# Heads 1 to 11 of a clustered attention: probabilities times values as one fp32 product

## The chip, the core and the metric

The program runs on one core of a Trainium2 chip. The metric is the device time of one execution in microseconds (us); the median of the runs is compared. Engines are named as in the profile: PE (TensorE matmul), PEld (its weight loads), DVE (VectorE), ACT (ScalarE), POOL (GpSimd), SP (SyncE, which issues most DMAs).

## What is computed

Three stages follow one another. The first is an attention in which a query sees only the keys whose nearest centroid is its own; the second is a two-layer block with a softmax-weighted unit (SoLU) and a layer norm; the third is a mixture of 8 experts with one expert a token. The change concerns the last line of the first function.

```python
B, H, S, D = 2, 8, 768, 64            # 16 heads in all
mask   = q_assign[:, :, :, None] == k_assign[:, :, None, :]
scores = np.where(mask, q @ k.T / 8, -1e9)
scores = scores - np.max(scores, axis=-1, keepdims=True)
attn   = np.exp(scores)
attn   = attn / (np.sum(attn, axis=-1, keepdims=True) + 1e-09)
return np.matmul(attn, v)             # (768 x 768) times (768 x 64), for each head

h  = x @ w_in;  solu = h * softmax(h);  y = layernorm(solu) @ w_out     # 1536 x 512 -> 1024 -> 512
out = gate * (relu(y_of_expert @ w1[e]) @ w2[e])                        # 8 experts, 512 -> 1024 -> 512
```

## The kernel before

Matmul operands are mostly kept as two fp16 halves: the high half is the value rounded to fp16, the low half is the remainder. A product of two such operands is three fp16 matmuls (high by high, high by low, low by high).

**The order.** All instructions of the attention and of the second stage are added to one `Plan`. Each `add(engine, cost, at, fn, reads, writes, ...)` gives a booked cost and a due time. `emit` plays a list scheduler: it takes at each step the ready operation with the lowest rank, where a rank is worked out from the due time, the length of the way to the end and a correction by kind and stretch from the table `LEAN`. The result is one fixed order for each engine's queue, SP's and POOL's too; the chip runs each queue in that order and waits at semaphores.

**The heads.** They go two at a time (a pair is one DMA of q and k, `prep`). Heads 0 and 12 to 15 go through `late`, in which probabilities are normalised by the row and turned by a DMA transpose. Heads 1 to 11 go through `head`:

- L499 and L502: for each of 6 blocks of 128 queries and 2 halves of the keys, one matmul of 384 columns into a PSUM bank and a DVE maximum over it. The maxima are turned (L511, L515, L517) and written as a row of q.
- L535 and L536: the transposed scores, keys by queries, one fp16 and one single-pass fp32 matmul (type fp32r) of 384 columns each, 12 pairs a head, into the PSUM tiles `psS`.
- L544: ACT takes the exponential of two blocks at a time (768 elements a partition), twice: once into fp16 (`ph`, shown as `pr`), once into fp32 (`pf`).
- L408 (`halves`): POOL subtracts, two instructions of 384 elements for each `pf`, and writes the low half `plo` (also shown as `pr`).
- L557 to L559 (`pv`): for each group of 128 queries, 6 key blocks by 3 fp16 matmuls of 65, 64 and 65 columns accumulate in one PSUM bank. Stationary are the probabilities, moving are the values; column 65 of the values is 1, so that the row sum comes out too. A head has two such groups of three, 6 calls of `pv`; the 11 heads have 66.
- L417 to L420 (`normalise`): DVE divides by the row sum and writes into `X`.

**The values.** L396 loads the fp32 values of a pair into `v32` (one buffer), L398 (ACT) makes their fp16 high half, L401 (DVE, twice a pair) the low half, in `V`.

**Beside them.** While the heads run, DVE, ACT and POOL also prepare the two weight matrices of the second stage (L612, L615 and L618 assemble fp32 words, L622 and L624 make halves, L631 on POOL). From about 180 us on, tiles of the second stage (L720 to L949) run between the later heads. The third stage begins at about 400 us.

Of the kernel before, what the change touches and what calls it, by code (L numbers as in the profile page):

```python
# [41 lines left out]
LEAN = {
    "act V": (0, 213.5, 0), "act bsm": (0, -40.4, 0), "act cw": (0, 0, 37), "act e": (0, -9.2, -1.9),
    "act hi": (221.8, 2.5, 0), "act hr": (1.3, 0, 0), "act lh": (0, 4.7, 0.4), "act ohT": (-1.5, 12.6, 0),
    "act pf": (0.1, -87.6, 0), "act rsm": (0, -0.2, 0), "act vh": (0, 6.2, 0), "act wf": (0, -2.6, 0),
    "act wgh": (3.6, 0, 0), "act wi": (113.4, 0, 0), "act wo": (-3.9, -4.3, 0), "act x1": (0, 6.6, 5.6),
    "act ys": (0, -3.4, -8.6), "dve V": (56.3, 3.7, 0), "dve X": (1.8, 0, 0), "dve acc": (0, -1.4, 0),
    "dve bsm": (0, 16.1, -0.1), "dve cbd": (5.6, 0, 0), "dve cw": (0, 0, 83.7), "dve e": (0, -2.8, -2.8),
    "dve eq": (7.7, -20.9, 0), "dve gs": (-0.7, 0, 0), "dve id": (-19.5, 0, 0), "dve ids": (0, 0, -5.1),
    "dve lo": (10.8, 0, 0), "dve loh": (0, -12, 0), "dve m2": (11.4, 0.6, 0), "dve mv": (4.7, 4.7, 0),  # L50
    "dve mx": (-0.2, 0.2, 0), "dve nm": (0, 6.3, 0), "dve nn": (2, 8.3, 0), "dve oh": (-2.6, -0.5, 0),
    "dve one": (1.6, 0, 0), "dve rn": (-3.7, 0, 0), "dve rr": (-10, 0, 0.5), "dve rsm": (0, -12.9, 0),
    "dve si": (0, 1.8, 0.9), "dve tri": (-6.2, 0, 0), "dve vl": (-6.3, 0.1, 0), "dve wf": (24.5, -1.2, 0),
    "dve wgl": (3.1, 0, 0), "dve wi": (6.9, 0, 0), "dve x1": (0, 0, 0.6), "dve ys": (0, 3.4, 3.4),
# [3 lines left out]
    "pool e": (0, 1.2, 0), "pool half": (6.6, 0, 0), "pool plo": (-0.5, 0, 0), "pool pn": (4.4, 0, 0),  # L58
# [136 lines left out]
def plan_attention(tc, plan, ctx, ps, qkT, vP, cent2, cst, cs, X, ident32, ident16):  # L195
# [3 lines left out]
    v32 = pa.tile([P, 2, NCH, D], F32, tag="v32", name="v32")  # L199
# [17 lines left out]
    ph, plo = [t[:, 0] for t in pr], [t[:, 1] for t in pr]  # L217
# [87 lines left out]
    lifted = ("QK1", 0, 2)

    def prep(p):
# [102 lines left out]
    def normalise(h, g, gv, t):  # L410
        def a3():
# [6 lines left out]
            out=r, in0=a3()[:, :, 64:65], scalar1=1e-9, scalar2=16.0, op0=ALU.add, op1=ALU.mult), reads=[gv], writes=[kr])  # L418
# [5 lines left out]
    def late(h):  # L424
# [10 lines left out]
        for c in range(NCH):  # L435
# [19 lines left out]
            old = ([] if first >= 7 else [(x, (2 * EH) % 3, i) for x in ("ph", "plo") for i in range(3)] if first < 3  # L455
# [861 lines left out]
```

## Time and profile before

| | us |
|---|---|
| median of 3 runs (lowest, highest) | 576.39 (576.3, 579.86) |
| the profiled execution | 580.83 |
| its span, first to last instruction | 579.1 |
| PE busy in the span | 506.7 (87%) |
| DVE busy | 417.3 (72%) |
| ACT busy | 368.1 (64%) |
| PEld busy | 326.7 (56%) |
| POOL busy | 278.3 (48%) |

The profiled execution lies 4.4 us above the median, and its span 2.7 us above it. Busy shares are means over stages with different limits, so they are read by stage. A busy PE is not a PE at its peak: the end of a matmul record is modelled, and records overlap. What a matmul costs its queue is read from the distance of the starts of two that follow each other.

### The profile page before, as it was taken

The numbers are of one execution on the slowest core, as the hardware profiler recorded it, in microseconds if no ns is written. First come the engines' busy times: TensorE is split into PE (matmuls) and PEld (weight loads), VectorE is DVE, ScalarE is ACT, GpSimd is POOL, SyncE is SP. The second block draws the span as 40 slices with busy tenths as digits, with TensorE's granted clock in tenths as the row PEclk, the third lists the DMA queues.
The fourth block names the chain that finished last, engine by engine and source line by source line (L and its number), as shares of the span: only waits on it lengthen the run. The fifth ranks groups of instructions, "written<-read, shape, count | busy, mean of one in ns | idle before, by whom it ended". The sixth has DMA issues, their size and how long they took to land.

```text
span 579.1 us, 13110 instructions
## 1 busy us (share of the span) xinstructions
PE 506.7 (87%) x4945; PEld 326.7 (56%) x4945; DVE 417.3 (72%) x976; ACT 368.1 (64%) x553; POOL 278.3 (48%) x292
## 2 busy tenths in 40 slices
PE   1478889889688898998889999988979999999995
PEld 1255666667565464654554445465727675675672
DVE  7499899999989899987755999963653445645110
ACT  3466788888767889986745989823544434635120
POOL 2057798999878758888752443520000101011001
PEclk9998899999979999999999999999979999999999
DMA  8898858796879799999999778948986573964300
GB/s 245 198 200 212 261 175 228 204 277 171 165 187 224 151 215 165 204 217 187 218 204 229 205 189 200 276 109 206 285 312 174 218 248 135 318 186 164 73 7 17
DMA packets 159340, 113.75 MB, mean 196 GB/s; under 512 B 126560, under 2 KB 135074, under 8 KB 159268
## 3 DMA queue, kind: packets, MB, share of 16 engines
q1 hardware_dynamic: 156660, 106.31, 74.8%
q0 software_dynamic: 2320, 6.32, 3.1%
q8 instruction: 46, 0.75, 0.5%
q14 instruction: 26, 0.21, 0.1%
q10 hardware_dynamic: 288, 0.16, 0.1%
HBM read 51.57 MB, written 17.11 MB: 119 GB/s over the span
## 4 chain that ended last, share of the span: by engine, by line
DVE 28%; issue 24%; DMA 23%; PE 14%; ACT 4%; POOL 4%; SPq 3%; POOLq 1%; ACTq 0%; DVEq 0%
DMA out_dram<-yo,ids 10%; DVE mm L502 6%; DMA pr<-pn 3%; DVE wf L615 2%; DVE hl L324 2%; PE psb L499 2%; DMA xs<-ys,si 2%; DVE mm L449 1%; DVE wf L618 1%; SPq L1024 1%; DMA wgs<-in_wg_dram 1%; DVE wf L612 1%; PE psS L446 1%; PE psS L445 1%; PE psS L535 1%
## 5 line engine op out<-in xcount | busy, mean ns | idle before, releaser
L408 POOL TENSOR_TENSOR pr<-pf,pr 128x384 f16<-128x384 f32 x168 | 173.0, 1060 | 54.9 <-ACT pr L460 27.6
L1084 POOL DMA_INDIRECT out_dram<-yo,ids x16 | 17.4, 1085 | 160.5 <-ACT yo L1081 153.5
L1057 PE MATMUL psb<-cxT,ah 128*128 128x256 f16 (+1 forms) x288 | 71.8, 261 | 1.5 <-DMA cxT<-xs 1.5
L1059 PE MATMUL psb<-cxT,al 128*128 128x256 f16 (+1 forms) x288 | 71.8, 261 | 0.9 <-PEq L1158 0.8
L1058 PE MATMUL psb<-cxT,ah 128*128 128x256 f16 (+1 forms) x288 | 71.8, 261 | 0.0
L502 DVE TENSOR_REDUCE mm<-psb 128x1 f32<-128x384 f32 x132 | 67.0, 546 | 4.9 <-PE psb L499 4.5
L1071 DVE SCALAR_TENSOR_TENSOR hl<-psb,hh 128x512 f16<-128x512 f32 x32 | 21.9, 689 | 58.3 <-ACT hh L1070 41.6
L991 DVE SCALAR_TENSOR_TENSOR al<-w,ah 128x1024 f16<-128x1024 f32 x32 | 40.5, 1279 | 29.2 <-ACT ah L990 29.1
L536 PE MATMUL psS<-QK 96*128 96x384 f32 x132 | 60.6, 494 | 0.0
L544 ACT ACTIVATE pf<-psS 128x768 f32<-128x768 f32 x66 | 53.1, 804 | 9.6 <-PE psS L536 5.7
L499 PE MATMUL psb<-QK 96*128 96x384 f32 x132 | 47.5, 416 | 13.3 <-DVE mm L502 9.8
L544 ACT ACTIVATE pr<-psS 128x768 f16<-128x768 f32 x66 | 52.6, 803 | 6.7 <-PE psS L536 6.2
L1076 PE MATMUL psb<-bh,hh 128*128 128x512 f16 x128 | 49.7, 388 | 3.2 <-ACT hh L1070 3.2
L1078 PE MATMUL psb<-bh,hl 128*128 128x512 f16 x128 | 49.8, 389 | 0.7 <-DVE hl L1071 0.7
L1077 PE MATMUL psb<-bl,hh 128*128 128x512 f16 x128 | 49.6, 388 | 0.0
L535 PE MATMUL psS<-QK 128*128 128x384 f16 x132 | 45.9, 348 | 1.7 <-ACT pr L544 1.0
L557 PE MATMUL psb<-V,pr 128*128 128x65 f16 x396 | 43.4, 196 | 3.6 <-DVE mm L502 3.1
L990 ACT ACTIVATE ah<-w 128x1024 f16<-128x1024 f32 x32 | 33.0, 1052 | 21.3 <-DMA w<-in_w_dram 20.5
L559 PE MATMUL psb<-V,pr 128*128 128x65 f16 x396 | 43.2, 194 | 1.1 <-POOL pr L408 1.1
L1070 ACT ACTIVATE hh<-psb 128x512 f16<-128x512 f32 x32 | 18.9, 592 | 38.6 <-PE psb L1059 38.4
L558 PE MATMUL psb<-V,pr 128*128 128x64 f16 x396 | 43.2, 197 | 0.0
L991 DVE SCALAR_TENSOR_TENSOR bl<-w,bh 128x1024 f16<-128x1024 f32 x32 | 39.0, 1230 | 5.8 <-ACT bh L990 4.6
(193 smaller groups left out, 1557.6 us busy)
## 6 DMA issues: line engine op xcount, KB each, us to landing
w<-in_w_dram SPq DMA_DIRECT2D x64, 512.0 KB
xs<-X SPq DMA_DIRECT2D x12, 516.0 KB
QK<-hr SPq DMA_DIRECT2D x16, 384.0 KB
QK<-hl SPq DMA_DIRECT2D x32, 192.0 KB
x<-in_qkT_dram SPq DMA_DIRECT2D x7, 768.0 KB
lT<-in_w_in_dram SPq DMA_DIRECT2D x8, 512.0 KB
lT<-in_w_out_dram SPq DMA_DIRECT2D x8, 512.0 KB
v<-in_vP_dram SPq DMA_DIRECT2D x8, 384.0 KB
```

Source lines behind the costliest of these rows:

```text
L408: nc.gpsimd.tensor_tensor(out=out[:, i], in0=a[:, i], in1=b[:, i], op=ALU.subtract)
L499: add("pe", 0.18, at(c - 10 + 0.25 * g), lambda c=c, g=g, w=w: nc.tensor.matmul(w.bank[:, :384], q1[:, c * P : (c + 1) * P], k1[:, g * 384 ...
L502: add("dve", 0.465, at(c - 9.9 + 0.25 * g), lambda c=c, g=g, w=w: nc.vector.tensor_reduce(out=m2[mm][:, c, g : g + 1], in_=w.bank[:, :384] ...
L535: nc.tensor.matmul(o, k2[:, ks], q2[:, qs], start=True, stop=False)
L536: nc.tensor.matmul(o, k1[:, ks], q1[:, qs], start=False, stop=True)
L544: add("act", 0.691, at(k + 0.5), lambda dst=dst, kb=kb: nc.scalar.activation(dst, ps[kb][:, :, :384], AF.Exp, scale=SC), reads=[kb], write ...
L991: run("dve", lambda: nc.vector.scalar_tensor_tensor(out=W[e][kl][:, gs], in0=box[0], scalar=64.0, in1=W[e][kh][:, gs], op0=ALU.mult, op1=A ...
L1057: nc.tensor.matmul(o, w["ah"][:, c, fs], x[:, 0, c, ts], start=(c == 0), stop=False)
L1058: nc.tensor.matmul(o, w["ah"][:, c, fs], x[:, 1, c, ts], start=False, stop=False)
L1059: nc.tensor.matmul(o, w["al"][:, c, fs], x[:, 0, c, ts], start=False, stop=(c == KC - 1))
L1076: nc.tensor.matmul(y, hh[:, f, i], w["bh"][:, f], start=(f == 0), stop=False)
L1078: nc.tensor.matmul(y, hl[:, f, i], w["bh"][:, f], start=False, stop=(f == FC - 1))
```

## The change

In `head` the fp16 exponential and the low half are gone: ACT writes one fp32 exponential per two blocks, straight into the space that `ph` and `plo` had, and `pv` multiplies the fp32 probabilities by the fp32 values in one matmul in place of three. The value tile has a column of ones of its own and two buffers; pairs 1 to 5 no longer make `V`. The scale 16 of the halves falls away in `normalise`. Heads 0 and 12 to 15 stay as they were, but for their waits: each wait for `ph` and `plo` is one for `ph` now. The booked cost of a `pv` is 0.8 in place of 0.5, and every entry of `LEAN` is another, so that all engines' orders are new. The diff, with most of `LEAN` and the two places of `late` left out:

```diff
@@ -38,28 +38,33 @@
 FIRST, LATE = 18, 8
+PV = 0.8
 MARKS = (48, 93,)
 LEAN = {
-    "act V": (0, 213.5, 0), "act bsm": (0, -40.4, 0), "act cw": (0, 0, 37), "act e": (0, -9.2, -1.9),
...
+    "act V": (-16.4, 37.6, 0), "act bsm": (0, 40.7, -22.6), "act cc": (169.2, 0, 0), "act cs": (54.1, 0, 0),
...
 }
@@ -196,7 +201,7 @@
     nc, add = tc.nc, plan.add
     pa = ctx.enter_context(tc.tile_pool(name="pa", bufs=1))
     x32 = pa.tile([P, 2, S], F32, tag="x32", name="x32")
-    v32 = pa.tile([P, 2, NCH, D], F32, tag="v32", name="v32")
+    v32 = ring(pa, "v32", 2, [P, 2, NCH, D + 1], F32)
     hl = ring(pa, "hl", 2, [P, 4, S], F16)
     hr = pa.tile([P, 2, S], F32R, tag="hr", name="hr")
     QK2 = ring(pa, "QK2", 2, [P, 2, S], F16)
@@ -214,7 +219,7 @@
     rn = mm_[:, 44:45]
     nmt = ring(pa, "nmt", 2, [NCH, P], F32R)
     pr = ring(pa, "pr", 3, [P, 2, NCH, 384], F16)
-    ph, plo = [t[:, 0] for t in pr], [t[:, 1] for t in pr]
+    ph = [t.rearrange("p a c t -> p (a c t)").bitcast(F32).rearrange("p (c t) -> p c t", c=NCH) for t in pr]
     E0, EH, E4 = 1, 12, 12 % 4
 
     def parts(t, n):
@@ -301,6 +306,7 @@
     for i in range(2):
         add("pool", 0.35, -90.0, lambda i=i: nc.gpsimd.memset(oh[i], 0.0), writes=[("oh", i)])
         add("pool", 0.1, -80.0, lambda i=i: nc.gpsimd.memset(V[i][:, :, :, 64:65], 1.0), writes=[("V1", i)])
+        add("pool", 0.1, -80.0, lambda i=i: nc.gpsimd.memset(v32[i][:, :, :, 64:65], 1.0), writes=[("v1", i)])
 
     lifted = ("QK1", 0, 2)
 
@@ -393,14 +399,17 @@
                     out=QK2[d2][64 * half : 64 * half + 64], in_=hl[b][r, 1:3] if half else hl[b][r, 0:4:3]),
                     reads=[(nm, b, t) for nm in ("hi", "lo") for t in range(2)] + ([lifted] if h == 1 or (h == 0 and 0) else []),
                     writes=[("QK2", d2, half)] + ([("neg", h)] if half and not E0 <= h < EH else []), data=0.2)
-        add("sp", 0.65, at(-10), lambda: nc.sync.dma_start(out=v32, in_=vP[p]),
-            reads=[("neg", 2 * p - 1)] if p else [], writes=["v32"], data=0.39)
-        add("act", 0.73, at(-2), lambda: nc.scalar.activation(V[b][:, :, :, 0:64], v32, AF.Copy, scale=16.0),
-            reads=["v32", ("oh", 0)], writes=[("V", b, 0), ("V", b, 1)])
+        v = v32[b][:, :, :, 0:D]
+        add("sp", 0.65, at(-8 if p else -10), lambda: nc.sync.dma_start(out=v, in_=vP[p]),
+            reads=[("neg", 2 * p - 1)] if p else [], writes=[("v32", b)], data=0.39)
+        if E0 <= 2 * p and 2 * p + 1 < EH:
+            return
+        add("act", 0.73, at(-2), lambda: nc.scalar.activation(V[b][:, :, :, 0:64], v, AF.Copy, scale=16.0),
+            reads=[("v32", b), ("oh", 0)], writes=[("V", b, 0), ("V", b, 1)])
         for j in range(2):
             add("dve", 0.47, at(-1), lambda j=j: nc.vector.scalar_tensor_tensor(
-                out=V[b][:, j, :, 65:129], in0=v32[:, j], scalar=16.0, in1=V[b][:, j, :, 0:64],
-                op0=ALU.mult, op1=ALU.subtract), reads=["v32"], writes=[("V", b, j)])
+                out=V[b][:, j, :, 65:129], in0=v[:, j], scalar=16.0, in1=V[b][:, j, :, 0:64],
+                op0=ALU.mult, op1=ALU.subtract), reads=[("v32", b)], writes=[("V", b, j)])
 
     def halves(out, a, b):
 
@@ -415,7 +424,8 @@
         r, kr = rr[u % 2], ("rr", u % 2)
         t0, hh = (h // H) * NCH + 3 * g, h % H
         add("dve", 0.07, t, lambda: nc.vector.tensor_scalar(
-            out=r, in0=a3()[:, :, 64:65], scalar1=1e-9, scalar2=16.0, op0=ALU.add, op1=ALU.mult), reads=[gv], writes=[kr])
+            out=r, in0=a3()[:, :, 64:65], scalar1=1e-9, scalar2=1.0 if E0 <= h < EH else 16.0, op0=ALU.add, op1=ALU.mult),
+            reads=[gv], writes=[kr])
         add("dve", 0.09, t, lambda: nc.vector.reciprocal(out=r, in_=r), writes=[kr])
         add("dve", 0.27, t, lambda: nc.vector.tensor_tensor(
             out=X[:, t0 : t0 + 3, hh * D : (hh + 1) * D], in0=a3()[:, :, 0:64], in1=r.to_broadcast([P, 3, D]), op=ALU.mult),
...
@@ -537,30 +547,20 @@
 
                 add("pe", 0.326, at(k + 0.3 * (c % 2)), sT,
                     reads=kqk + [("QK1", d, 4 + g), ("QK2", d2, 0), ("QK2", d2, 1)], writes=[kb])
-                fb = n % 3
-                old = free.get(u, [])
                 if c % 2:
-                    for dst, key in ((ph[ub][:, c - 1 : c + 1], ("ph", ub, c // 2)), (pf[fb], ("pf", fb))):
-                        add("act", 0.691, at(k + 0.5), lambda dst=dst, kb=kb: nc.scalar.activation(
-                            dst, ps[kb][:, :, :384], AF.Exp, scale=SC), reads=[kb], writes=[key] + (old if key[0] == "ph" else []))
-                if c % 2:
-                    add("pool", 1.6, at(k + 0.8), lambda c=c, fb=fb, ub=ub: halves(
-                        plo[ub][:, c - 1 : c + 1], pf[fb], ph[ub][:, c - 1 : c + 1]),
-                        reads=[("pf", fb), ("ph", ub, c // 2)], writes=[("plo", ub, c // 2)])
+                    add("act", 0.691, at(k + 0.5), lambda c=c, ub=ub, kb=kb: nc.scalar.activation(
+                        ph[ub][:, c - 1 : c + 1], ps[kb][:, :, :384], AF.Exp, scale=SC),
+                        reads=[kb], writes=[("ph", ub, c // 2)] + free.get(u, []))
             gv = Hold()
             for qc in range(3):
                 def pv(qc=qc, ub=ub, gv=gv):
                     A = gv.bank[:, qc * 65 : qc * 65 + 65]
-                    v = V[b]
                     qs = slice(qc * P, (qc + 1) * P)
                     for c in range(NCH):
-                        nc.tensor.matmul(A, ph[ub][:, c, qs], v[:, j, c, 0:65], start=(c == 0), stop=False)
-                        nc.tensor.matmul(A[:, :64], ph[ub][:, c, qs], v[:, j, c, 65:129], start=False, stop=False)
-                        nc.tensor.matmul(A, plo[ub][:, c, qs], v[:, j, c, 0:65], start=False, stop=(c == NCH - 1))
-
-                add("pe", 0.5, at(3 * g + (2.9 + 0.1 * qc if h == EH - 1 else 4.5 + 0.8 * qc)), pv,
-                    reads=[("ph", ub, i) for i in range(3)] + [("plo", ub, i) for i in range(3)]
-                    + [("V", b, j), ("V1", b)], writes=[gv], get=None if qc else gv)
+                        nc.tensor.matmul(A, ph[ub][:, c, qs], v32[b][:, j, c], start=(c == 0), stop=(c == NCH - 1))
+
+                add("pe", PV, at(3 * g + (2.9 + 0.1 * qc if h == EH - 1 else 4.5 + 0.8 * qc)), pv,
+                    reads=[("ph", ub, i) for i in range(3)] + [("v32", b), ("v1", b)], writes=[gv], get=None if qc else gv)
             normalise(h, g, gv, at(3 * g + 6.3))
 
     for p in range(NPAIR):
```

## Rows read from the trace of the kernel before

**Rows 1.** Windows: us, busy PE, PEld, DVE, ACT, POOL, clock, DMA share.
```profile
60.00:150.00 90.00, 80.85 (x1136) 61.28 (x1136) 87.75 (x185) 75.97 (x105) 83.00 (x80) 0.98 0.78 226
150.00:180.00 30.00, 23.71 (x280) 17.40 (x279) 27.70 (x49) 22.52 (x33) 24.90 (x23) 0.83 0.74 165
180.00:240.00 60.00, 53.19 (x620) 32.13 (x619) 55.40 (x138) 51.50 (x87) 45.33 (x47) 1.00 0.96 184
240.00:310.00 70.00, 61.95 (x755) 36.99 (x754) 51.26 (x182) 48.41 (x78) 50.44 (x59) 1.00 1.13 205
310.00:410.00 100.00, 94.98 (x754) 51.38 (x751) 77.25 (x257) 67.24 (x125) 32.47 (x33) 1.00 0.80 208
```

**Rows 2.** Groups by line, 60-150 us: xcount | busy, mean ns | idle.
```profile
L408 POOL TENSOR_TENSOR pr<-pf,pr 128x384 f16<-128x384 f32 x80 | 84.5, 1088 | 7.0 <-ACT pf L544 5.5 <-PE psb L499 1.3
L502 DVE TENSOR_REDUCE mm<-psb 128x1 f32<-128x384 f32 x84 | 42.4, 546 | 1.8 <-PE psb L499 1.6
...
L499 PE MATMUL psb<-QK 96*128 96x384 f32 x82 | 27.1, 380 | 6.2 <-DVE mm L502 5.5 <-DMA QK<-ohT 0.3 <-ACT nmt L517 0.2
...
L324 DVE SCALAR_TENSOR_TENSOR hl<-x,hl 128x768 f16<-128x768 f32 x6 | 8.5, 1432 | 0.0
...
L624 DVE SCALAR_TENSOR_TENSOR il<-wf,ih 128x512 f16<-128x512 f32 x6 | 6.4, 1066 | 0.1
L615 DVE SCALAR_TENSOR_TENSOR wf<-lT,wf 128x512 int32<-128x512 int32 x5 | 5.9, 1176 | 0.0
L618 DVE SCALAR_TENSOR_TENSOR wf<-lT,wf 128x512 int32<-128x512 int32 x5 | 5.2, 1044 | 0.0
...
L401 DVE SCALAR_TENSOR_TENSOR V<-v,V 128x384 f16<-128x384 f32 x6 | 4.6, 774 | 0.0
```

**Rows 3.** Groups by line, whole span.
```profile
L544 ACT ACTIVATE pf<-psS 128x768 f32<-128x768 f32 x66 | 53.1, 804 | 9.6 <-PE psS L536 5.7 <-POOL pr L408 3.6
...
L398 ACT ACTIVATE V<-v 128x768 f16<-128x768 f32 x8 | 6.7, 844 | 0.0
```

**Rows 4.** Single lines: xcount, ns min/median/max, first and last start.
```profile
L324 DVE SCALAR_TENSOR_TENSOR hl<-x,hl x16: 928/1053/1671, 7.7 to 204.6; 128x768 f16<-128x768 f32 x16
L615 DVE SCALAR_TENSOR_TENSOR wf<-lT,wf x16: 693/1256/1402, 14.9 to 221.8; 128x512 int32<-128x512 int32 x16
L618 DVE SCALAR_TENSOR_TENSOR wf<-lT,wf x16: 676/914/1401, 15.6 to 223.8; 128x512 int32<-128x512 int32 x16
L624 DVE SCALAR_TENSOR_TENSOR il<-wf,ih x8: 675/900/1403, 26.0 to 149.9; 128x512 f16<-128x512 f32 x8
```

**Rows 5.** Timeline, PE, 84-90 us: start, duration, line.
```profile
84.81 0.32 PE L535 MATMUL psS<-QK 128*128 128x384 f16 x1
...
85.15 0.34 PE L535 MATMUL psS<-QK 128*128 128x384 f16 x1
...
87.42 0.19 PE L557 MATMUL psb<-V,pr 128*128 128x65 f16 x1
...
87.94 0.19 PE L559 MATMUL psb<-V,pr 128*128 128x65 f16 x1
87.96 0.42 PE L499 MATMUL psb<-QK 96*128 96x384 f32 x1
```

**Rows 6.** Timeline, PEld, 85.8-86.5 us.
```profile
85.94 0.30 PEld L499 LDWEIGHTS psb<-QK 96*128 96x128 f32 x2
86.40 0.10 PEld L535 LDWEIGHTS <-QK 128*128 128x128 f16 x1 [0.16 <-issue]
```

**Rows 7.** Single lines, transposes on PE: columns as in rows 4.
```profile
L365 PE MATMUL psb<-ident,oh x48: 217/219/330, 13.7 to 227.1; 128*128 128x128 f16 x48
L515 PE MATMUL psb<-ident,mm x11: 271/273/402, 42.6 to 187.9; 128*6 128x128 f32 x11
L297 PE MATMUL psb<-ident,pf x1: 444/444/444, 6.1 to 6.1; 128*128 128x128 f32 x1
```

**Rows 8.** DMA queue of SP: packets, MB, share of 16 engines.
```profile
q1 hardware_dynamic: 156660, 106.31, 74.8%
```

More of the change, by code (lines that the diff above doesn't have):

```diff
@@ L40 @@
 FIRST, LATE = 18, 8
+PV = 0.8
 MARKS = (48, 93,)
 LEAN = {
-    "act V": (0, 213.5, 0), "act bsm": (0, -40.4, 0), "act cw": (0, 0, 37), "act e": (0, -9.2, -1.9),
[L44 to L52, printed above, removed]
@@ L53 @@
-    "dve si": (0, 1.8, 0.9), "dve tri": (-6.2, 0, 0), "dve vl": (-6.3, 0.1, 0), "dve wf": (24.5, -1.2, 0),
-    "dve wgl": (3.1, 0, 0), "dve wi": (6.9, 0, 0), "dve x1": (0, 0, 0.6), "dve ys": (0, 3.4, 3.4),
[3 rows of a table removed]
-    "pool e": (0, 1.2, 0), "pool half": (6.6, 0, 0), "pool plo": (-0.5, 0, 0), "pool pn": (4.4, 0, 0),
[4 rows of a table removed]
+    "act V": (-16.4, 37.6, 0), "act bsm": (0, 40.7, -22.6), "act cc": (169.2, 0, 0), "act cs": (54.1, 0, 0),
+    "act cw": (0, 0, 409.8), "act e": (0, 0, 126.2), "act hi": (-50.9, 163.3, 0), "act hr": (8.7, 3.8, 0),
@@ new lines @@
+    "act lh": (0, 256, -0.4), "act nmt": (-5.8, -20.4, 0), "act ohT": (-21.2, -92.1, 0), "act pf": (-0.5, 17.8, 0),
+    "act ph": (-33.8, 123.2, 0), "act pn": (0.6, -1.6, 0), "act rsm": (0, 18.2, -13.9), "act vh": (-17.4, -74.5, 0),
+    "act wf": (9.4, 266.8, 0), "act wi": (-2.9, 0, 0), "act wo": (25.1, -25.6, 0), "act x1": (0, 266.1, -0.6),
+    "act ys": (0, 9.9, 36.2), "dve V": (28.7, 0, 0), "dve X": (91.2, 94, -47.8), "dve acc": (0, 5.2, 15.9),
+    "dve bsm": (0, -3.8, -517.5), "dve cbd": (-6.2, 0, 0), "dve cnt": (0, 0, 57.9), "dve cw": (0, 0, -23),
@@ new lines @@
+    "dve e": (0, 403.7, 1.3), "dve eq": (28.5, 40.5, 0), "dve gs": (-30.8, 0, 0), "dve id": (-3.9, 0, 0),
+    "dve ids": (0, 0, 33.9), "dve lo": (0, -6.8, 0), "dve loh": (0, 34.9, -86.3), "dve m": (17.7, -74.5, 0),
+    "dve m2": (168.2, -0.7, 0), "dve mv": (0, 81.6, 0), "dve mx": (61, 3.7, 0), "dve nm": (29.6, -59.3, 0),
+    "dve nn": (-0, -13.5, 0), "dve oh": (0.1, 7.9, 0), "dve one": (63.3, 0, 0), "dve rn": (22.6, 0, 0),
+    "dve rr": (153.9, -24.5, -1), "dve rsm": (0, 123.6, -102.1), "dve si": (0, 79.1, 1.8), "dve tie": (-111.7, 0, 0),
@@ L63 @@
+    "dve tri": (-31.6, 0, 0), "dve vl": (-34.6, -234.9, 0), "dve wf": (617.7, -1, 0), "dve wgl": (-1, 0, 0),
[4 rows of a table added]
+    "pool X": (-35.4, 0, 0), "pool bsm": (0, -9, 45), "pool e": (0, 92.7, -7.4), "pool half": (4.6, 0, 0),
+    "pool id32": (-8.3, 0, 0), "pool oh": (-1.1, 0, 0), "pool pn": (11.1, -0.6, 0), "pool ring": (0, -27, 8.3),
+    "pool rn": (3.5, 0, 0), "pool v1": (25, 0, 0), "pool wo": (-20.9, 48.1, 0), "pool ysi": (0, 4.1, 14.7),
[4 rows of a table added]
 }
@@ L454, in late @@
                 reads=[("nm", h % 2, c)], writes=[("nn", h % 2, c), ("m2", h % 2, c, 1)])
-            old = ([] if first >= 7 else [(x, (2 * EH) % 3, i) for x in ("ph", "plo") for i in range(3)] if first < 3
+            old = ([] if first >= 7 else [("ph", (2 * EH) % 3, i) for i in range(3)] if first < 3
                    else [("more", (first - 3) // 2)])
@@ L464, in late @@
                 reads=[("pf", fb), ("pn", ib, 0)], writes=[("pn", ib, 1)])
-            old = [(x, (2 * EH + 1 + ub) % 3, i) for x in ("ph", "plo") for i in range(3)] if first < 6 else []
+            old = [("ph", (2 * EH + 1 + ub) % 3, i) for i in range(3)] if first < 6 else []
             add("sp", 1.69, at(o + 0.7), lambda c=c, ib=ib, ub=ub: nc.sync.dma_start(
```

15 rows, old and new, of the table LEAN are left out of this document.

## The prediction

> **What bounds the kernel now.** I read the busy time by stage first, because shares of the whole span mix stages. From 60 to 150 us, where the heads run almost alone, DVE is busy 87.75 of 90 us and POOL 83.0, while PE's records cover 80.9 and ACT 76.0 [rows 1]. Then I read the groups by line in that stretch. It holds 84 DVE maxima of L502 and 84 is 7 x 12, so exactly 7 heads pass, one in 12.86 us. DVE waits there almost for nobody, while PE's L499 waits 5.5 us for DVE's L502 to free a bank [rows 2]. POOL's subtractions of L408 take 1088 ns each; 12 a head are 13.1 us, as long as a head [rows 2]. So two engines are full at once. The single lines tell that they are full partly of each other: the DVE operations with two inputs in SBUF have minima of 0.68 to 0.93 us [rows 4] and means of 1.04 to 1.43 us in this stretch [rows 2], while L502, which reads PSUM, keeps 546 ns. The reader is to see that a DVE operation beside L408 pays for L408.
>
> PE has to be read by starts. A pv call of 18 fp16 matmuls runs from 87.42 to 87.96, 0.54 us, 30 ns a matmul; a pair of L535 and L536 takes 85.15 - 84.81 = 0.34 us [rows 5], so one matmul of 384 columns about 0.17. A head's PE work is then 12 x 0.17 + 12 x 0.34 + 6 x 0.54 = 9.4 us. The 128 other matmuls of the stretch (1136 less 7 x 144 [rows 1, 5]) at 30 ns add 0.55 a head: 9.9 of 12.86 us. PE has some 3 us a head to spare, although its records look full.
>
> Later the limits change. From 180 to 240 us PE is busy 53.2 of 60 and DVE 55.4; from 240 to 310 the DMA share is 1.13; from 310 to 410 PE is busy 95.0 of 100 [rows 1].
>
> **The change part by part.** *POOL* loses 11 x 12 = 132 of its L408, at 1088 ns 144 us [rows 2]. *ACT* loses the 66 exponentials into pf, 53.1 us, and 5 of 8 conversions of the values, 5 x 0.844 = 4.2 us [rows 3]; the pv calls need not wait for POOL behind ACT any more. POOL and ACT then have room everywhere in the heads, so these two terms count only through DVE.
>
> *DVE* loses L401 for five pairs; 6 of them are in the stretch, 4.6 us [rows 2]. The contention goes with L408: mean less minimum is 6 x (1432 - 928) + 6 x (1066 - 675) + 5 x (1176 - 693) + 5 x (1044 - 676) ns = 3.0 + 2.3 + 2.4 + 1.8 = 9.6 us [rows 2, 4]. POOL keeps L631 and some work of the second stage, so between 0 and 9.6 us comes back; I take all of it for this stretch, since hardly any other POOL work lies in it. DVE goes from 87.75 to 73.6 us for 7 heads, 10.5 us a head.
>
> *PE* loses 66 calls at 0.54 us and gets 66 calls of six fp32 products each. No row shows such a product, and this is the open price. An fp32 transpose of 128 columns takes 273 ns where an fp16 one takes 219 [rows 7]: 54 ns more, so fp32 columns pass at half the pace. A load of weights in 4-byte form takes longer too: two of them merged take 0.30 us, one fp16 load 0.10 [rows 6]. If a single one takes 0.19, the second began 0.11 us after the first, so one load holds the path for 0.11. That gives three prices. With all loads hidden and one load a product, 6 x 0.11 = 0.66 us a call. With two loads a product, one for the upper and one for the lower bits, 6 x 0.22 = 1.3 us. With nothing overlapped, six times the only fp32 matmul with 128 x 128 weights in the trace, 444 ns [rows 7], 2.7 us. I take 0.8, near the lower end. The reason is the kernel's own bookings, which agree with the starts within 8%: 0.5 booked against 0.54 for the old pv call, 0.326 against 0.34 for a pair [rows 5]; the new call is booked at 0.8. That is weak, so both ends stay in the range, the third as a tail.
>
> The Trainium skill speaks against the change here. Its page "FP8 and Floating Point Precision", section "TensorE Precision Notes", says a true fp32 product is four passes through the array; by the 30 ns of a pass that is an estimate of 0.12 us a product, 0.72 a call, and the sum below would come out some 5 us lower. Its page "TensorE: Matmul & The Clock Gate", section "Weight-path perf modes", says that fast weight load is off for fp32 weights. The slower fp32r loads agree with that, but no run here shows how many loads an fp32 product needs.
>
> *The sum per head.* PE: 9.9 - 3.24 + 4.8 = 11.5 us. DVE: 10.5. PE becomes the longer one. Where PE is the limit, from 310 to 410 us, it reaches 95% [rows 1], so a head takes 11.5 / 0.95 = 12.1 in place of 12.86 us, and 7 heads give 5.3 us. From 150 to 180 us DVE is at 27.7 of 30 [rows 1]; two heads at 0.75 give 1.5. From 180 to 240 us the last three gain a DVE that was full and pay 3 x 1.6 us on a PE that had 6.8 us idle; I put a gain of 2 there, as much again as 0.75 x 3. After 240 us nothing changes. The sum is 5.3 + 1.5 + 2 = 9 us: the span goes from 579.1 to 570 us. The median lies 2.7 us below the profiled span, so 567 us.
>
> *What costs nothing.* The value load writes runs of 64 fp32 into rows of 65, so 128 packets of a load become 128 x 12. At the queue's mean, 0.748 x 16 x 579.1 us / 156660 = 44 ns a packet [rows 8], 1408 more are 62 us on 16 engines, 3.9 us a load at most. It is due 8 steps before its heads, booked at 1.9 us each, and has two buffers now; in the stretch DMA is at 0.78 [rows 1]. Were that cover gone, a pair's first pv call would be late by up to 4 us. It moves two steps later on SP's queue, past other loads of QK; it is one instruction as before. The two new memsets lie at the start, where POOL is idle. The new order of all queues has no price in any row; by the DVE idle time left in the stretch, 2.25 us of 90 [rows 1], a better order alone was worth little before, and a worse one is bounded by nothing that I can read.
>
> **The rivals.** *Loads bind the fp32 products* (slower). With two loads a call takes 1.3 us and a head's PE work is 9.9 - 3.24 + 7.8 = 14.5, at 95% 15.2 us: 2.4 more for each of 7 heads, 17 us, and in 180 to 240 us three heads bring 13.7 us of PE work into 6.8 us of idle time, some 7 more. The median would be 576.4 + 24 = 600. For it speaks the longer fp32 load [rows 6], against it only the booking. It decides from a PE head of 0.95 x 12.86 = 12.2 us on, a call of 0.93 us, 155 ns a product. The Trainium skill's rule on fast weight load, above, is this case.
>
> *The gain is given back* (no change). The heads end earlier, but what follows from 240 to 310 us hangs on DMA transposes at a DMA share of 1.13 [rows 1], which the change doesn't touch. If the second stage and heads 12 to 15 take up only half the lead, 4 or 5 us stay: 572 us, and 576 if nothing stays.
>
> *More relief.* At 0.66 us a call a head is 10.6 / 0.95 = 11.2 us on PE, DVE still below; 1.7 x 7 = 12, with the later stages about 18: 558 us.
>
> *Nothing overlaps.* At 2.7 us a call 66 calls bring 143 us; with 3 us a head spare, about 110 stay: 686 us.
>
> **How the numbers follow.** The forecast, 567 us, has a chance of 0.40, its own range 560 to 574, by calls between 0.7 and 0.9 us. More relief 0.08, given back 0.14, loads bind 0.33, nothing overlaps 0.05. A measurement of this kernel can tell about 1% from no change, 5.8 us. Faster than 570.6 are nine tenths of the forecast and all of more relief: 0.44. Slower than 582.2 are nearly all of loads bind, and nothing overlaps: 0.37. Between them 0.19. Four fifths lie from 555 us (below more relief) to 602 us (the two-load case with its 600); what is left out is nothing overlaps, the outer part of loads bind, and a little below.
>
> **What would show it.** Right: in the stretch of the heads L324, L615, L618 and L624 fall to their minima, a head takes 12 us, the starts of the new line's matmuls lie 0.13 us apart, and PE rather than DVE ends the waits. Wrong: starts 0.2 us or more apart, with weight loads back to back on PEld and DVE and ACT waiting for PE; or heads done by 225 us and an unchanged start of the third stage, which is the lead given back. The forecast falls if a product costs over 155 ns, whatever DVE does.

## The result: 1.2% slower, and TensorE full

| | before | after |
|---|---|---|
| median, runs of one chip | 578.12 us (576.30 to 580.41) | 585.80 us (585.38 to 587.14, 4 runs) |
| profiled span | 579.1 us | 585.4 us |

The ratio is 1.012, 95% interval 1.0072 to 1.0168. Here and below a median is of all runs, while a ratio leaves out runs over 1.5% above the fastest of the same kernel, so a ratio can differ from the quotient of the medians. The forecast was 567 us and faster; the sign is wrong (slower had a chance of 0.37), and the time lies within 555 to 602, which reached so far for "loads bind".

The windows of after (columns as in [rows 1]):
```profile
60.00:150.00 90.00, 89.97 (x783) 81.25 (x782) 67.15 (x157) 43.85 (x57) 0.00 (x0) 1.00 0.70 194
150.00:180.00 30.00, 28.70 (x250) 24.95 (x249) 21.71 (x51) 17.33 (x24) 2.31 (x2) 1.00 1.07 203
180.00:240.00 60.00, 59.05 (x491) 44.77 (x489) 46.66 (x122) 40.57 (x67) 16.53 (x16) 1.00 0.94 189
240.00:310.00 70.00, 67.50 (x805) 41.49 (x805) 56.29 (x194) 55.60 (x88) 53.30 (x62) 1.00 1.19 219
310.00:410.00 100.00, 90.50 (x676) 46.14 (x674) 73.38 (x263) 63.17 (x121) 33.45 (x35) 0.98 0.82 179
```
From 60 to 150 us PE is busy 89.97 of 90 us where it was at 80.85; DVE fell from 87.75 to 67.15 and POOL from 83.0 to nothing [rows 1]. The full engine is another one.

The groups by line of after, 60 to 150 us (L512 is L502 of before, L330 is L324; L560 is the new product):
```profile
L560 PEld LDWEIGHTS psb<-v,pr 128*128 128x128 f32 x427 | 52.7, 192 | 0.3
L560 PE MATMUL psb<-v,pr 128*128 128x65 f32 x428 | 51.9, 270 | 0.0
L512 DVE TENSOR_REDUCE mm<-psb 128x1 f32<-128x384 f32 x73 | 38.5, 553 | 14.9 <-PE psb L509 14.3
...
L330 DVE SCALAR_TENSOR_TENSOR hl<-x,hl 128x768 f16<-128x768 f32 x6 | 5.5, 950 | 0.0
...
L618 DVE SCALAR_TENSOR_TENSOR wf<-lT,wf 128x512 int32<-128x512 int32 x6 | 4.1, 680 | 0.0
...
L624 DVE SCALAR_TENSOR_TENSOR il<-wf,ih 128x512 f16<-128x512 f32 x5 | 3.4, 682 | 0.0
L615 DVE SCALAR_TENSOR_TENSOR wf<-lT,wf 128x512 int32<-128x512 int32 x5 | 3.4, 677 | 0.0
```
Three things are to be seen. The 73 maxima are 6.08 heads, one in 14.8 us; before it was 7, one in 12.86 [rows 2]. The two-input DVE operations fell to 677 to 950 ns from 1044 to 1432 [rows 2], to their minima. And 428 records of L560 for 6 heads are 72 a head, where a head has 36 products: each product is two loads of weights and two matmuls.

A stretch of after's timeline on PE (start, duration, line), and after it the same stretch on PEld:
```profile
99.74 0.27 PE L525 MATMUL psb<-ident,mm 128*6 128x128 f32 x1
99.86 1.45 PE L560 MATMUL psb<-v,pr 128*128 128x65 f32 x12
101.14 0.33 PE L545 MATMUL psS<-QK 128*128 128x384 f16 x1
```
```profile
99.75 1.42 PEld L560 LDWEIGHTS psb<-v,pr 128*128 128x128 f32 x12
101.03 0.15 PEld L545 LDWEIGHTS <-QK 128*128 128x128 f16 x1
```
A call of six products runs from 99.86 to 101.14, 1.28 us, with twelve loads back to back beside it. Over the whole trace the median distance from one start of L560 to the next is 112 ns; two are 224 ns a product. Only the first two matmuls of a call lie closer, 59 ns apart by the median of the 59 calls that stand alone, so a call takes 1.285 us and not 12 x 0.112 = 1.34.

The list of waits from 60 to 150 us names PE in its longest entries (engine, line, waited for: us, times, longest):
```profile
ACT pr L551 <- PE psS L546: 43.4, 30, 4.3
DVE mm L512 <- PE psb L509: 14.3, 20, 1.5
DVE mm L426 <- PE psb L560: 5.9, 8, 2.4
```

Three single lines tell how the loss travels to the end: the last write of a head's output, the last scatter of the second stage, the first product of the third. Before, then after:
```profile
L420 DVE TENSOR_TENSOR X<-psb,mm x32: 342/348/359, 61.5 to 310.6; 128x192 f32<-128x192 f32 x32
...
L868 POOL DMA_INDIRECT xs<-ys,si x12: 967/1036/2096, 252.0 to 389.6; - x12
...
L1057 PE MATMUL psb<-cxT-1_5556,ah x32: 216/219/219, 384.9 to 390.1; 128*128 128x128 f16 x32
```
```profile
L430 DVE TENSOR_TENSOR X<-psb,mm x32: 345/350/358, 51.9 to 309.8; 128x192 f32<-128x192 f32 x32
...
L868 POOL DMA_INDIRECT xs<-ys,si x12: 968/1037/1950, 261.1 to 400.6; - x12
...
L1057 PE MATMUL psb<-cxT-1_4545,ah x32: 219/219/314, 398.1 to 403.8; 128*128 128x128 f16 x32
```
The attention ends as before, at 310 us, although its heads were slower; but the second stage ends 11 us later and the third begins 13.2 us later. Of these the third stage gives 7 back: the span grows by 6.3.

### The profile page after: what moved, and what is told of

Same layout as the page of the kernel before. It is cut to its first block, busy times and chain, and to the rows that moved or that the text cites. A ratio compares the mean times of both kernels' runs of the same rounds, so it can differ in the third digit from the quotient of the medians.

```text
span 585.4 us, 11936 instructions
## 1 busy us (share of the span) xinstructions
PE 538.8 (92%) x4549; PEld 376.0 (64%) x4549; DVE 386.5 (66%) x966; ACT 322.6 (55%) x482; POOL 139.7 (24%) x162
## 3 DMA queue, kind: packets, MB, share of 16 engines
q1 hardware_dynamic: 167924, 106.31, 77.7%
## 5 line engine op out<-in xcount | busy, mean ns | idle before, releaser
L560 PEld LDWEIGHTS psb<-v,pr 128*128 128x128 f32 x792 | 97.1, 192 | 1.3
L560 PE MATMUL psb<-v,pr 128*128 128x65 f32 x792 | 95.3, 271 | 0.0
L551 ACT ACTIVATE pr<-psS 128x768 f32<-128x768 f32 x66 | 53.0, 809 | 67.3 <-PE psS L546 67.0
L512 DVE TENSOR_REDUCE mm<-psb 128x1 f32<-128x384 f32 x132 | 69.4, 551 | 26.7 <-PE psb L509 25.8
L546 PE MATMUL psS<-QK 96*128 96x384 f32 x132 | 59.6, 485 | 0.4 <-DMA QK<-nmt 0.4
L991 DVE SCALAR_TENSOR_TENSOR al<-w,ah 128x1024 f16<-128x1024 f32 x32 | 38.6, 1220 | 25.9 <-ACT ah L990 25.6
L1078 PE MATMUL psb<-bh,hl 128*128 128x512 f16 x128 | 48.5, 379 | 0.8 <-DVE hl L1071 0.8
L1076 PE MATMUL psb<-bh,hh 128*128 128x512 f16 x128 | 48.5, 379 | 0.2 <-ACT hh L1070 0.2
L631 POOL TENSOR_TENSOR wol<-wf,woh 128x512 f16<-128x512 f32 x8 | 9.3, 1158 | 157.5 <-ACT wf L629 157.5
L417 POOL TENSOR_TENSOR pr<-pf,pr 128x384 f16<-128x384 f32 x36 | 32.8, 939 | 36.2 <-ACT pr L470 35.9
L746 PE MATMUL psb<-ih,xT 128*128 128x512 f16 x96 | 36.6, 381 | 5.1 <-DMA xT<-x 5.1
```

Of the source, the lines that this page charges most:

```text
L512: add("dve", 0.465, at(c - 9.9 + 0.25 * g), lambda c=c, g=g, w=w: nc.vector.tensor_reduce(out=m2[mm][:, c, g : g + 1], in_=w.bank[:, :384] ...
L546: nc.tensor.matmul(o, k1[:, ks], q1[:, qs], start=False, stop=True)
L551: add("act", 0.691, at(k + 0.5), lambda c=c, ub=ub, kb=kb: nc.scalar.activation(ph[ub][:, c - 1 : c + 1], ps[kb][:, :, :384], AF.Exp, scal ...
L560: nc.tensor.matmul(A, ph[ub][:, c, qs], v32[b][:, j, c], start=(c == 0), stop=(c == NCH - 1))
L991: run("dve", lambda: nc.vector.scalar_tensor_tensor(out=W[e][kl][:, gs], in0=box[0], scalar=64.0, in1=W[e][kh][:, gs], op0=ALU.mult, op1=A ...
L1076: nc.tensor.matmul(y, hh[:, f, i], w["bh"][:, f], start=(f == 0), stop=False)
```

## The experiments

Times are medians; the ratio is to the kernel before on the same chip, with its 95% interval. The theory after the result was: two weight loads of 0.112 us bind each product (the rival "loads bind"). Against it stood that the product was dear for another reason, that the new order was at fault, and that even a cheap product would not have brought the forecast.

**Is a product's price its columns or its loads?** cols130 multiplies two key blocks' values at once, 130 columns in place of 65; the columns that are too many go unused.
```diff
-  nc.tensor.matmul(A, ph[ub][:, c, qs], v32[b][:, j, c], ...)
+  w = 2 if c < NCH - 1 else 1
+  nc.tensor.matmul(gv.bank[:, qc * 130 : qc * 130 + 65 * w], ph[ub][:, c, qs], v32[b][:, j, c : c + w], ...)
```


> The changed kernel, but each fp32 product for the first five of six key blocks streams 130 columns of values (this block's 65 and the next block's 65, the second half into an unread part of the bank) in place of 65. If a product is bound by its two weight loads of 0.112 us each, the distance of the starts stays near 0.112 us, a head stays at 15.0 us and the time at 586 us. If it is bound by its columns, the starts of the wide ones go to about 0.22 us, a call from 1.34 to about 2.5 us, a head to 22 us, and the time to 630 us or more.

584.34 us, the median of four runs from 578.36 to 589.16: too spread to compare with the changed kernel's 585.80 to 1%, but far from the 630 us of the columns. Its groups by line, 60 to 150 us, and one call in its timeline:
```profile
L560 PEld LDWEIGHTS psb<-v,pr 128*128 128x128 f32 x431 | 53.2, 190 | 0.3
L560 PE MATMUL psb<-v,pr 128*128 128x130 f32 x359 | 46.1, 274 | 0.0
L512 DVE TENSOR_REDUCE mm<-psb 128x1 f32<-128x384 f32 x73 | 38.5, 554 | 14.9 <-PE psb L509 14.2
```
```profile
95.00 1.45 PE L560 MATMUL psb<-v,pr 128*128 128x130 f32 x12
96.29 0.33 PE L545 MATMUL psS<-QK 128*128 128x384 f16 x1
```
Twice the columns cost nothing: 1.29 us a call, 73 maxima again, the median distance of starts 111 ns. So the columns are not the price. What is left is the loads, which follow each other 112 ns apart in both kernels, with 0.3 us of idle time among 431; a fixed cost of the matmul itself was not tried apart from them. The margin is small: the first two matmuls of a call, 59 ns apart at 65 columns, are 113 ns apart at 130. I read these two distances as the time of the columns, and at 130 they are as long as a load.

**What would a cheap product have brought?** half_product is the changed kernel with key blocks 0, 2 and 4 alone, so half of each sum is left out: six loads a call, and 0.62 us a call by the median.
```diff
-  for c in range(NCH):
+  for c in range(0, NCH, 2):
```


> The changed kernel, order and all, but a pv call multiplies only key blocks 0, 2 and 4: half of the keys are left out of the product, and a call costs 0.67 us in place of 1.34, a little under the price of the forecast. If the price was the only step that failed, a head takes 11 to 12 us and the time is 555 to 567 us. If a lead of the heads is given back later, the heads are as fast and the time is 573 to 580 us.

573.1 us, ratio 0.9879 (0.9838 to 0.992). From 60 to 150 us, its window, one group and two waits:
```profile
60.00:150.00 90.00, 81.05 (x579) 68.92 (x579) 67.08 (x163) 45.16 (x60) 0.00 (x0) 0.87 0.77 217
```
```profile
L512 DVE TENSOR_REDUCE mm<-psb 128x1 f32<-128x384 f32 x77 | 39.9, 551 | 9.3 <-PE psb L509 9.3
L546 PE MATMUL psS<-QK 96*128 96x384 f32 x76 | 37.9, 532 | 0.1
```
```profile
ACT pr L551 <- PE psS L546: 34.5, 29, 3.1
...
PEld psb L509 <- DMA QK<-ohT: 3.4, 1, 3.4
```
Half the price is worth 2.4% against the changed kernel by the two ratios, 14 us, and the loss turns into a gain: the price of the product is the cause of the loss. But the heads are one in 90 x 12 / 77 = 14.0 us, not 11.2 as "more relief" had it, with no engine full: ACT waits for PE, PE for a load of QK, and the granted clock falls to 0.87, a mean of stretches at 2.4 and at 1.2 GHz, so that L546 takes 532 ns in place of 474. Two slices and what follows each show when it falls:
```profile
65.00:70.00 5.00, 1.76 (x13) 1.41 (x12) 0.81 (x4) 1.77 (x2) 0.00 (x0) 1.00 0.95 281
70.00:75.00 5.00, 4.84 (x22) 4.50 (x20) 3.89 (x7) 3.83 (x6) 0.00 (x0) 0.58 0.18 49
135.00:140.00 5.00, 2.63 (x17) 2.00 (x17) 2.93 (x8) 1.73 (x4) 0.00 (x0) 0.90 0.27 56
140.00:145.00 5.00, 5.00 (x21) 4.60 (x20) 2.13 (x6) 1.85 (x3) 0.00 (x0) 0.50 0.90 274
```
PE is busy 1.76 and 2.63 of 5 us, and then runs at 0.58 and 0.50 of its clock.

four_f16 takes the second way to a cheap call: fp16 probabilities, four fp16 matmuls a block (two by the values' halves, two by zeros), 24 a call. The low half of the probabilities is left out.
```diff
-  nc.tensor.matmul(A, ph[ub][:, c, qs], v32[b][:, j, c], ...)
+  nc.tensor.matmul(A, x, V[b][:, j, c, 0:65], ...)
+  nc.tensor.matmul(A[:, :64], x, V[b][:, j, c, 65:129], ...)
+  for z in range(2): nc.tensor.matmul(A, x, zt, ...)
```


> The changed kernel with another product: the exponential goes to fp16, and a key block is four fp16 matmuls (the values' high and low half, and two with zeros as the moving operand); the low half of the probabilities is left out, and pairs 1 to 5 make V again. A pv call costs about 0.72 us, so this is the changed kernel at about the price that the forecast took. If the forecast's chain holds and only the price was off, a head takes 11.5 to 12 us and the time is 558 to 567 us. If a lead of the heads is given back later, the heads are as fast but the time stays at 573 to 578 us.

583.58 us, ratio 1.0029 (0.9989 to 1.0068). A call takes 0.75 us by the median, about the price of the forecast. No engine is full in its window either: PE 83.58 of 90, DVE 75.53.
```profile
60.00:150.00 90.00, 83.58 (x1338) 65.95 (x1336) 75.53 (x182) 51.34 (x68) 0.00 (x0) 0.96 0.77 215
```
Its heads gained (83 maxima, 13.0 us), and the last output is written at 305.3 us, 4.5 earlier than in after; by the two ratios the time is 0.9% shorter, 5 us.

**What is the relief alone worth?** fix_no_low is the kernel before with its order entry by entry, without the second exponential and without POOL's subtraction; PE multiplies by zeros where the low half stood (that part of the product is left out), so its work is unchanged.
```diff
-  add("act", 0.691, at(k + 0.5), lambda dst=dst, kb=kb: nc.scalar.activation(
+  add("act", 0.691, at(k + 0.5), lambda dst=dst, kb=kb, key=key: key[0] == "ph" and nc.scalar.activation(
...
-  add("pool", 1.6, at(k + 0.8), lambda c=c, fb=fb, ub=ub: halves(
-      plo[ub][:, c - 1 : c + 1], pf[fb], ph[ub][:, c - 1 : c + 1]),
+  add("pool", 1.6, at(k + 0.8), lambda: None,
...
-  nc.tensor.matmul(A, plo[ub][:, c, qs], v[:, j, c, 0:65], ...)
+  nc.tensor.matmul(A, ph[ub][:, c, qs], zt, ...)
```


> The kernel before with every engine's order kept as it is, but in heads 1 to 11 the second exponential and POOL's subtraction are not issued, and the third matmul of a key block streams zeros. It leaves the low half of the probabilities out. If DVE and POOL held the heads through each other, a head goes from 13.2 to 11 to 11.5 us and the time to 562 to 568 us. If the lead is given back later, the heads are as fast, but the attention still ends near 305 to 311 us and the time is 573 to 578 us. If the loss of the run without the low half came from removing the work and not from its new order, this run is at 585 us or more too.

574.64 us, ratio 0.994 (0.9904 to 0.9975).
```profile
60.00:150.00 90.00, 79.02 (x1126) 61.24 (x1124) 75.83 (x185) 53.09 (x70) 0.00 (x0) 0.96 0.84 229
```
```profile
ACT pr L550 <- PE psS L542: 24.2, 23, 4.9
DVE mm L508 <- PE psb L505: 8.0, 11, 2.8
...
PEld psb L505 <- DMA QK<-ohT: 4.0, 2, 3.4
```
DVE fell by 12 us of 90, POOL to nothing, at PE's old work, and 3.5 us came of it. (The halves of the values are still made here, so their part of the relief is not in this number.) So being full did not bind the heads alone. The list of waits now names each engine waiting for another and for the loads of QK, with none of them full, which points to the chain through one head; that chain was not tried by itself. no_low_half, the same edit with the order found by the program from the old corrections, shows how much hangs on that order:

> The kernel before without the second exponential and without POOL's subtraction in heads 1 to 11; the third matmul of a key block takes zeros as the moving operand, so PE's work is as before. It leaves the low half of the probabilities out. If DVE and POOL bound the heads through each other, L324, L615, L618 and L624 fall to their minima of 0.68 to 0.93 us, a head goes from 13.2 to 11 to 11.5 us, and the time to 562 to 568 us. If the gain is given back later, the time stays within 1% of 578 us.

588.74 us, ratio 1.0115 (1.0055 to 1.0174), slower with less work: the maxima of three heads start at 59, 70 and 79 us, those of the next at 110.

**What is the order worth?** oldlean is the changed kernel with the corrections of the kernel before (`LEAN` alone differs).

> The changed kernel with the order corrections of the kernel before. If the order has no part in the result, heads still take 15 us and the time is 586 us within 4 us. If the new order is what keeps the loss small (the second stage's work put into PE's gaps), the time goes to 592 us or more; if the new order is what costs, it goes to 580 us or less.

613.66 us, ratio 1.0586 (1.0539 to 1.0634); the last output is written at 341.8 us. But those corrections with new bookings make an order that is neither kernel's. The clean comparison is fix_fp32c: the kernel before, entry by entry, with the fp32 product in heads 1 to 11 and three buffers for values.
```diff
-  v32 = pa.tile([P, 2, NCH, D], F32, tag="v32", name="v32")
+  v32 = ring(pa, "v32", 2, [P, 2, NCH, D + 1], F32)
...
+  W3 = v32 + [V[1].rearrange("p j c d -> p (j c d)").bitcast(F32)...]
...
-  nc.tensor.matmul(A, ph[ub][:, c, qs], v[:, j, c, 0:65], start=(c == 0), stop=False)
-  nc.tensor.matmul(A[:, :64], ph[ub][:, c, qs], v[:, j, c, 65:129], start=False, stop=False)
-  nc.tensor.matmul(A, plo[ub][:, c, qs], v[:, j, c, 0:65], start=False, stop=(c == NCH - 1))
+  nc.tensor.matmul(A, ph[ub][:, c, qs], W3[(h // 2) % 3][:, j, c], ...)
```


> The order of the kernel before, the fp32 product in heads 1 to 11, three buffers for the values, every call reading the buffer of its own pair (fix_fp32b read one buffer for all). Theory A (two weight loads bind each product, and the new order is worth something of its own): about 15 us a head and 590 to 596 us. Rival B (in fix_fp32 and fix_fp32b the calls waited for value loads, the order is worth nothing): 584 to 587 us, as the changed kernel.

592.12 us, ratio 1.0241 (1.0182 to 1.0299); its last output:
```profile
L437 DVE TENSOR_TENSOR X<-psb,mm x32: 343/348/358, 59.2 to 321.6; 128x192 f32<-128x192 f32 x32
```
In the old order the loss reaches the attention's end, 321.6 us for 310.6, and the span, +10.0. The new order brings the attention back to 309.8 but leaves more of the second stage behind it.

**Where is the price paid?** fix_2to7b and fix_8to11b are fix_fp32c with the product in heads 2 to 7 or 8 to 11 alone (`WIDE` names the heads, all others keep the halves).

> The fp32 product in heads 2 to 7 alone, halves in heads 1 and 8 to 11, in the order of the kernel before, every call reading its own pair's buffer. If the price is paid where TensorE becomes full (60 to 150 us): about 15 us a head there and 588 to 592 us. If it were spread evenly: six elevenths of what fix_fp32c loses, 585 to 588 us.

593.83 us, ratio 1.025 (1.0192 to 1.0307).

> The fp32 product in heads 8 to 11 alone, halves in heads 1 to 7, in the order of the kernel before, every call reading its own pair's buffer. If TensorE's idle time from 150 to 240 us covers the price: 576 to 581 us, as the kernel before. If spread evenly: four elevenths of what fix_fp32c loses, 583 to 586 us. If the relief of VectorE counts for more there, as fix_8to11 (575.9) would have it: 572 to 576 us, and a version faster than both kernels.

586.4 us, ratio 1.0118 (1.0062 to 1.0174). Windows of fix_8to11b:
```profile
150.00:180.00 30.00, 27.40 (x236) 23.53 (x237) 19.75 (x47) 14.21 (x20) 1.93 (x3) 0.83 0.76 159
180.00:240.00 60.00, 58.30 (x481) 41.99 (x478) 45.22 (x120) 38.38 (x65) 15.31 (x15) 1.00 0.86 179
```
PE's idle time after 150 us does not cover the price: four heads bring 24 x (1.28 - 0.54) = 18 us of PE work into the 13 us that PE was idle from 150 to 240 us [rows 1], and by the ratio they cost 6.8 us (3.6 to 10.1). Four elevenths of fix_fp32c's 13.3 us, 4.8, lie within that, so these four alone do not rule out an even price. But the parts do not add up: 2.5% and 1.2% alone, 2.4% together (head 1 is in neither part). Six heads alone cost as much as eleven; which wait makes it so is not shown.

Four earlier kernels of this kind, fix_fp32, fix_fp32b, fix_2to7 and fix_8to11, read another pair's values in part of the products, so their calls may have waited for loads that were not theirs:

> The changed kernel's instructions for heads 1 to 11 in the order of the kernel before, which was made for the work of before (a wide exponential, no second one, no subtraction, one fp32 product, V only for pairs 0, 6 and 7). It is the change without its new order. If the price of the product alone decides, PE is full at 15 us a head, 1.8 us more than before for each of 7 heads, and with the later heads on a PE that is nearly full the time is 590 to 600 us. If the changed plan with the old corrections (613 us) was slow for the product itself, it is near 613 us; if the new order brought nothing, it is 586 us.

> The kernel before in its own order, with the fp32 product in heads 1 to 11 and a third buffer for the values, so that each head gets its own. Theory A (two weight loads of 0.112 us bind each product; the order found anew is worth something of its own): a head takes about 15 us and the time is 590 to 595 us, some 8 us above the changed kernel. Rival B (in the run without a third buffer the calls waited for value loads, and the new order is worth nothing): 584 to 587 us, as the changed kernel.

> As the run before it, but the fp32 product only in heads 2 to 7, the halves in heads 1 and 8 to 11, all in the order of the kernel before. If the price is paid where TensorE has become full (60 to 150 us): a head takes about 15 us there against 13.2, and the time is 588 to 592 us, 10 us or more above the kernel before. If the price were spread evenly over the eleven heads: six elevenths of it, about 586 us.

> The fp32 product only in heads 8 to 11, the halves in heads 1 to 7, in the order of the kernel before. If idle TensorE time from 150 to 240 us covers the price there: 576 to 581 us, as the kernel before. If the price were spread evenly: four elevenths of it, about 584 us. If the relief of VectorE and GpSimd counts more there: below 575 us.

They took 594.09, 603.56, 601.08 and 575.87 us. The last looked like a version faster than both kernels; with its own values it is not.

**Was the order made for a wrong price?** rebooked is the changed kernel with `PV = 1.34` and corrections found by a short search of mine for that booking.

> The changed kernel with the product booked at 1.34 us a call in place of 0.8 and an order found for that booking. If the loss came from an order made for the wrong price: below 580 us, at or under the kernel before. If the loss is the weight loads themselves, which no order removes: 583 to 590 us, and a head still takes about 15 us.

611.9 us, from 595.2 to 620.1 in four runs: slower, by how much is not well measured. That this order is poor says nothing against a better one; a better order for the true price stays open.

**What holds the attention's end?** fix_half_turn keeps the kernel before and its order, but heads 0 and 12 to 15 transpose only the upper half of their probabilities by DMA (the lower half is left out, zeros stand in its matmul).
```diff
-  nc.sync.dma_start(out=pT_[ub][:, c % 3], in_=pn_[ib], transpose=True)
+  nc.sync.dma_start(out=pT_[ub][:, c % 3, :NCH], in_=pn_[ib][:, :S], transpose=True)
```


> The kernel before in its order, but in heads 0 and 12 to 15 the DMA transpose turns only the high half of the probabilities, half of the bytes, and the third matmul of a key block streams zeros; the low half of those heads is left out. In six runs the end lay 268 to 277 us behind the end of the attention. If the DMA transposes of heads 12 to 15 hold the attention's end, and this holds the rest, the attention ends 5 to 12 us earlier and the time falls by as much, to 566 to 574 us. If they don't, both stay within 2 us.

571.85 us, ratio 0.9871 (0.9816 to 0.9926).
```profile
240.00:310.00 70.00, 67.45 (x764) 40.28 (x762) 54.86 (x189) 49.18 (x80) 48.17 (x56) 0.98 0.80 161
```
The DMA share falls from 1.13 [rows 1] to 0.80, the last output is written at 302.9 in place of 310.6 us, and the span is 8.3 us shorter. It leaves work out, so it is no version to use, but by its ratio it is worth 1.3%, against 0.6% for the relief of DVE and POOL in fix_no_low, although the two intervals overlap.

| kernel | first maximum starts | last output starts | span | span less last output |
|---|---|---|---|---|
| before | 27.6 | 310.6 | 579.1 | 268.5 |
| fix_no_low | 26.9 | 302.4 | 568.6 | 266.2 |
| fix_half_turn | 25.3 | 302.9 | 570.8 | 267.9 |
| fix_fp32c | 26.0 | 321.6 | 589.1 | 267.5 |
| fix_2to7b | 29.3 | 327.0 | 594.3 | 267.3 |
| fix_8to11b | 30.8 | 317.6 | 585.7 | 268.1 |
| after | 27.3 | 309.8 | 585.4 | 275.6 |
| cols130 | 24.4 | 306.3 | 578.8 | 272.5 |
| half_product | 25.9 | 301.6 | 574.9 | 273.3 |
| four_f16 | 26.7 | 305.3 | 581.9 | 276.6 |

The six kernels in the old order have the same 266 to 269 us behind the attention, the four in the new order 272 to 277. In one order the end is the attention's end plus a constant, and a microsecond of the attention's end counts in full.

Each row is one execution, and the first maximum starts anywhere from 24.4 to 30.8 us, before any head's product has run; why was not tried. Counted from it, the last output comes after 283.0 us in before, 295.6 in fix_fp32c, 297.7 in fix_2to7b, 286.8 in fix_8to11b, 277.6 in fix_half_turn, 275.5 in fix_no_low (its fastest execution, 4.2 us below its median) and 282.5 in after. So 3.2 of the 7.0 us by which the attention of fix_8to11b ends later were there before its wide products.

## Why the prediction was wrong, step by step

- **Relief of DVE and POOL: right as work, wrong as time.** The two-input operations fell to their minima, POOL to nothing and DVE to 67.15 us for 6.08 heads, 11.0 a head against the 10.5 forecast. But fix_no_low prices the relief, without the values' part, at 0.6%, 3.5 us: PE's work there is the old 9.9 us a head by the prediction's count, and DVE is busy 75.83 of 90 us, so either would have allowed far more. So a call at about the forecast's price does not give the forecast, 0.984 of 576.4 us: four_f16 with 0.75 us, which makes the halves of the values again, is at 1.0029, and half_product with 0.62 us at 0.9879. Two full engines were read as the bound, and something else, most likely the chain through one head, was nearly as long.
- **The price of a call: the step that failed.** 0.8 us was taken on the strength of the kernel's own booking; it is 1.28, so the term of 6 x 0.8 = 4.8 us a head is 7.7. The load time was read rightly, 0.11 us [rows 6]; what the booking hid is that there are two for each product. Of the bounds 0.66, 1.3 and 2.7 the middle one was the case, and the forecast stated its own limit at 155 ns a product; 224 were measured. The Trainium skill's page "FP8 and Floating Point Precision", section "TensorE Precision Notes", speaks of four passes; the estimate by it, 0.12 us a product, was half of what the trace shows. By the columns alone it agrees, two matmuls at 59 ns; the loads make it 0.224. The estimate lay below the 0.8 us a call taken, so it spoke for the change, not against it. The rule of the Trainium skill's page "TensorE: Matmul & The Clock Gate", section "Weight-path perf modes", that fast weight load is off for fp32, pointed the right way: the load records of L560 take 192 ns, those of the fp16 weights of L342 in the same stretch 96.
- **"Loads bind": right in mechanism, too large in size.** A PE head of 14.5 us and a pace of 15.2 were forecast; the pace is 14.8. The 24 us became 13 in the old order and 7 to 8 in the new. The ladder is by ratios: relief -0.6% (fix_no_low), price +3.0% (fix_fp32c against it), order -1.2% (the changed kernel against fix_fp32c), together +1.2%. (The 3.0% is the price less the values' part of the relief.) The price is 66 x (1.28 - 0.54) = 49 us of PE work; 17 us of it, 3.0% of 579, reach the end. That the rest went into PE's spare 3 us a head, 11 x 3 = 33 us, is an estimate that fits. My sum set the new pace against 12.86 us and so charged too much: from the first maximum of head 1 to that of head 11, ten heads, before takes 27.6 to 167.5 us, 14.0 a head, and after 27.3 to 177.0, 15.0. That is 1 us a head, not 2.4. The forecast's own sum counts 7 + 2 + 3 = 12 heads of 11; by their pv matmuls 7.0, 1.5 and 2.5 lie in the three stretches.
- **The order: mis-sized.** It was held to be worth little by DVE's 2.25 idle us. It is worth 1.2% here, and a poor one cost 1.15% (no_low_half) and 5.9% (oldlean).
- **"The gain is given back": in part.** No constant share is lost after 240 us, as the table shows; a gain is passed on. What goes is a shift between attention and second stage, 4 to 10 us more behind the attention's end in the new order. The third stage gives some back in the kernel after: from 420 to 440 us PE was busy 15.99 of 20 us before at a clock of 0.83, and 18.88 at 1.00 after. The stage starts 13.2 us later in after, so the two stretches hold different work; why it took less time was not tried.
- **What costs nothing: right.** The value loads came out as worked out, 8 x 1408 = 11264 packets more than in [rows 8], at 0.777 x 16 x 585.4 / 167924 = 43 ns each, and no pv call waits for one.
```profile
q1 hardware_dynamic: 167924, 106.31, 77.7%
```

## What to carry to other kernels

Before an fp16 split is replaced by an fp32 product, count its loads: a product was two loads of 112 ns, at 65 columns and at 130 alike, against three fp16 matmuls at 30 ns with 65. At 130 the columns take as long as the loads, and no run here is wider. Two engines that are full beside each other are not yet the bound: take the work away in the old order and see what the time does, before pricing the relief. Where a program finds its order from bookings, compare kernels in one fixed order, or the order's own 1 to 6% is read as the change's.

## What the runs showed of the hardware that was not expected

- An fp32 product with 128 x 128 weights leaves two LDWEIGHTS and two MATMUL records, 111 to 112 ns apart at 65 and at 130 columns alike. Only the first two matmuls of a call tell the widths apart, 59 and 113 ns.
- Less PE work can come with a lower clock: 1.00 from 60 to 150 us in after, with PE busy 89.97 us, and 0.87 in half_product with 81.05, where the fp32r matmul takes 532 in place of 474 ns. There it falls after PE has waited: PE is busy 1.76 of 5 us from 65 to 70 us, and the clock of the next 5 us is 0.58. The busy time of a long stretch does not tell it: from 150 to 180 us the clock is 0.83 with 27.40 of 30 us busy in fix_8to11b and 1.00 with 28.70 in after.
